# Later fetches for v and the routing constants, and half of the first k copies moved to VectorE

## Chip, cores and metric

The kernel runs on one core of a Trainium2 chip. The metric is the time of one execution on the device in microseconds (us); smaller is better.

## What is computed

Three layers in a row, on a batch of B=4 sequences of S=576 rows.

```python
# 1. attention: 8 heads of 64; heads 0-3 see 32 earlier rows, heads 4-7 every fourth of 128 earlier rows
scores = where(mask[h], q @ k.T / sqrt(64), -1e9)
x = softmax(scores) @ v                      # heads side by side: [B, S, 512]
# 2. mixture of experts: one of 8 experts per row, chosen by a gate
logits = x @ w_gate; local = sigmoid(x @ w_local)
e[s] = argmax(logits[s]) if s == 0 or local[s] < 0.5 else e[s-1]
x[s] = softmax(logits[s])[e] * (relu(x[s] @ w1[e]) @ w2[e])     # 512 -> 1024 -> 512
# 3. last layer: convolution over 5 rows as a gate
gate = sigmoid(sum(conv_w[k] * shifted(x, 4 - k)))
out = (gate * (x @ w_val)) @ w_out
```

## The kernel before

The attention is cut into eight **items**, `it` 0 to 7. An item is one pair of heads for two sequences (`bl` 0 and 1). Items 0 and 1 are heads 0 and 1, then 2 and 3, of sequences 0 and 1; item 2 is the first pair of the strided heads. An item is cut into five **groups**, and the outer loop (L1041) counts groups, `t` = 5 * `it` + `gi`. Within one `t` the work of several groups is interleaved in a hand-written order; each engine runs its instructions strictly in that order, so whatever stands behind a waiting instruction on the same engine waits too.

For one group: `stage_a` multiplies q by a block-diagonal k (`kbd`) on TensorE into PSUM (tile `s`, L561) and VectorE adds the mask and takes the row maximum (`sm`, `mx`, L569); `stage_sub` subtracts the maximum on GpSimd (L577); `stage_exp` is on ScalarE (L584); two groups later `stage_b` transposes the result (`pt`, `ph`); three later `stage_c` multiplies by v (`o`, L630), and the result goes to `xsb`. `stage_d` and `stage_l` transpose it (`tpx`) and accumulate the gate's logits (`lp`).

Ahead of an item its q and k must be transposed. `load_qk(it, bl)` issues one transfer for q (`qraw`) and one for k (`kraw`), 288 KB each, on SyncE's queue, SP. `side` packs q for the transposes (`qside`), on VectorE for items 0 and 1 (L480) and on GpSimd from item 2 on (L482), in two halves for each `bl`. `qraw` has two buffers, so a transfer for one item waits until `side` has read the one two transfers before it. `transpose_qk` transposes eight units per item: for q, VectorE copies PSUM to `qT` (L531, L529); for k, ScalarE makes two copies per unit, one for even rows (`e` = 0) and one for odd (`e` = 1), from the two halves of the PSUM partitions into `kbd` (L545, L542). Item 0's units 0 to 3 are made before the loop, 4 and 5 at `t` = 0 and 6 and 7 at `t` = 1; the k units are 2, 3, 6 and 7, so item 0 has eight k copies.

v is loaded by `load_v`, a generator with one transfer at each step: for heads 0 to 3 of a sequence four transfers of 144 KB, one for each head. Before the loop heads 0 and 1 of sequences 0 and 1 are sent; heads 2 and 3 are put into the list `vq`, from which `send` takes up to six transfers a group at `t` % 10 < 2 and four otherwise. Their first readers are `shift_v` of item 1 on ScalarE at `t` = 6 and 9 and `stage_c` of item 1. The constants come in four parts (`consts_in`); part 2 holds the masks of the strided heads and is fetched at `t` = CONSTS[0], part 3 holds the routing's constants, 933 columns of 4 bytes on 128 partitions or 466.5 KB, and is fetched at `t` = CONSTS[1]. `tables` is a generator that makes three sets of tables from part 3 on VectorE: `triu` and `lane` (L197, L198), then `lanes` (L200), then `cols` and `sv` (L202, L203); one set is made at each `t` in PREP. The routing that reads them starts at `t` = START = 25.

`busy(n)` issues n matmuls of no use, to keep TensorE at work: 40 at the start and FILL[0] and FILL[1] after k units 1 and 3. Some ten lines of the loop set the order on SP; at the end of one `t` it is:

```python
if t == 2:
    load_qk(2, 0)
if (gi == 1 and it and it + 2 < 8) or t == 3:
    load_qk(it + 2, 1)
...
if gi == 3 and it + 3 < 8:
    load_qk(it + 3, 0)
for n in (2, 3):
    if t == CONSTS[n - 2]:
        consts_in(nc.sync, n)
if t in PREP:
    next(prep, None)
...
left = send(vq, 6 if t % 10 < 2 else 4)
```

After the attention the experts' matmuls and the last layer follow; they are not touched.

Of the kernel before, what the change touches and what calls it, by code (L numbers as in the profile page):

```python
# [50 lines left out]
TILES = 5  # L51
VB = 3
BUSY = 40
FILL = (6, 16)
SPLIT = ((33, 34), (33, 34), (34, 36), (37, 38), (38, 39), (39, 42), (41, 43), (41, 42), (45, 46), (47, 48), (48, 50), (51, 52), (52, 57), (55, 59), (57, 61), (61, 63))
GATHERS = (37, 38, 38, 40)
TURNS = (39, 40, 40, 43)
UP = (42, 43, 44, 44, 45, 46, 46, 47)
EXPERT2 = 33
CONSTS = (4, 7)  # L60
LATE = ((0, 1, 0, 1, 0, 1, 0, 1, 0, 1, 0, 1, 0, 1, 0, 1), (1, 1, 1, 1, 1, 1, 1, 2, 1, 1, 1, 1, 1, 1, 1, 2), (1, 1, 1, 1, 1, 1, 1, 1, 1, 1, 1, 1, 1, 1, 1, 1), (0, 1, 1, 1, 1, 1, 1, 1, 0, 1, 1, 1, 1, 1, 1, 1), (0, 1, 1, 0, 1, 1, 0, 1, 1, 0, 1, 1, 0, 1, 1, 1), (0, 1, 0, 1, 0, 1, 0, 1, 1, 0, 1, 0, 1, 0, 1, 1), (0, 0, 1, 0, 1, 0, 1, 0, 0, 1, 0, 1, 0, 1, 0, 1))
RINGS = ((1, 1), (2, 1), (2, 3), (3, 0), (1, 0), (2, 0), (0, 0), (0, 0))
PREP = (10, 18, 22)
PLACES = (1, 0, 0, 2)
EVACUATE = 2
START = 25
# [93 lines left out]
def attention_moe_conv_kernel(ctx: ExitStack, tc: tile.TileContext, q, k, v, w_gate, w_local, w1, w2, w_val, conv_w, w_out, consts, out):  # L160
    nc = tc.nc
    V, A, G, T = nc.vector, nc.scalar, nc.gpsimd, nc.tensor
# [10 lines left out]
    def consts_in(eng, n):  # L173
        eng.dma_start(out=cst[:, cuts[n] : cuts[n + 1]], in_=consts[:, cuts[n] : cuts[n + 1]])
# [253 lines left out]
    if True:  # L428
# [28 lines left out]
        def pair(it):  # L457
            return it // 4, PR[it // 4][it % 4]

        def load_qk(it, bl):  # L460
            bp, pr = pair(it)
            b = 2 * bp + bl
            for nm, src in (("q", q), ("k", k)):
                tj, tp = TJ[pr >= 2], TP[pr >= 2]
                r = ld.tile([tp, 2, tj, HD], F32, tag=f"{nm}raw", name=f"{nm}raw{it}_{bl}", bufs=2 if nm == "q" else 4)
                rows = src[b, 2 * pr : 2 * pr + 2].rearrange("h (p j) d -> p h j d", j=tj)
                nc.sync.dma_start(out=r, in_=rows)
                raw[it, bl, nm] = r
# [40 lines left out]
        def psum(ring, it, shape, nm):  # L509
            pool, tag = ((trp, "tr"), (pp, "pt"), (sp, "s"), (op, "o"))[ring[it == 7]]  # L510
            return pool.tile(shape, F32, tag=tag, name=nm)

        def transpose_qk(it, unit):
            bp, pr = pair(it)
            bl, n2, jj = unit // 4, (unit // 2) % 2, unit % 2
            nm = "qk"[n2]
            if unit == 0:
                qk[it] = (qt.tile([P, 2, S], F32, tag="qT", name=f"qT{it}"), kbd[it % 2])
            dil = pr >= 2
            tj, tp = TJ[dil], TP[dil]  # L520
            hj = tj // 2
            ps = psum(RINGS[6 + n2], 0 if jj == 0 else 7, [P, hj, tp], f"tp{nm}{it}_{unit}")
            qT, (kb, _) = qk[it]
            if nm == "q":
                for rr in range(hj):
                    T.transpose(ps[:, rr, :], sides[it, bl][:, hj * jj + rr, :], ident[:tp, :tp])
                t = qT[:, bl, :]
                if dil:
                    V.tensor_copy(out=t.rearrange("c (r p two) -> c r p two", r=4, two=2)[:, :, :, jj], in_=ps)  # L529
                else:  # L530
                    V.tensor_copy(out=t.rearrange("c (p j) -> c p j", j=tj)[:, :, hj * jj : hj * jj + hj], in_=ps.rearrange("c r p -> c p r"))  # L531
                later.tick()
                return
            h = jj
            for m in range(hj):
                T.transpose(ps[:, m, :], raw[it, bl, "k"][:, h, 2 * m : 2 * m + 2, :].rearrange("p e d -> p (e d)"), ident[:tp, :tp])
            t = kb[HD * h : HD * h + HD, bl, h, :]
            for e in range(2):
                half = ps[HD * e : HD * e + HD]
                if dil:  # L540
                    to = t.rearrange("c (m e p two) -> c e two m p", m=2, e=2, two=2)[:, e]
                    A.copy(out=to, in_=half.rearrange("c (two m) p -> c two m p", two=2))  # L542
                else:
                    to = t.rearrange("c (p m e) -> c e p m", m=hj, e=2)[:, e]
                    A.copy(out=to, in_=half.rearrange("c m p -> c p m"))  # L545

        def scores(nm):
            return sp.tile([P, 2, 2, KB], F32, tag="s", name=nm)
# [451 lines left out]
        vq, xq, evs, xs = [], [], {}, [[], []]  # L1000
# [9 lines left out]
        def v_of(m):  # L1010
            b, dil = 2 * (2 * (m // 2) // 4) + m % 2, pair(2 * (m // 2))[1] >= 2
            return load_v(b, dil)

        with tc.manual_schedule():
# [4 lines left out]
            v0, v1 = v_of(0), v_of(1)  # L1019
# [1 line left out]
            send([v1], 2)  # L1021
            load_qk(1, 0)
            load_qk(1, 1)
            vq += [v0, v1]

            def busy(n):
                ps = op.tile([P, P], F32, tag="o", name="busy")
                for _ in range(n):
                    T.matmul(ps, lhsT=ones16, rhs=ones16, start=True, stop=True)
# [4 lines left out]
            for u in range(4):  # L1034
                transpose_qk(0, u)
                if u % 2:
                    busy(FILL[u // 2])
            for half in range(2):
                side(0, 1, half)
            prep = tables()  # L1040
            for t in range(NG + 5):  # L1041
                it, gi = divmod(t, 5)
                if t < NG:
                    stage_a(t)
                    if t < 2:
                        for u in (4 + 2 * t, 5 + 2 * t):
                            transpose_qk(0, u)
                    elif t < 5:
                        for u in ([0, 1], [2, 3], [4, 5, 6, 7])[t - 2]:
                            transpose_qk(1, u)  # L1050
                    elif it + 1 < 8:
                        for u in units[gi]:
                            transpose_qk(it + 1, u)
                    stage_sub(t)
# [35 lines left out]
                    nc.gpsimd.dma_start(out=wg[:, :, E : E + 1], in_=w_local.rearrange("(c p) e -> p c e", p=P))  # L1090
                if t == 2:
                    load_qk(2, 0)
                if (gi == 1 and it and it + 2 < 8) or t == 3:
                    load_qk(it + 2, 1)
                if gi in (1, 2) and it + 2 < 8 and it:
# [9 lines left out]
# [5 lines that stand above are left out]
# [518 lines left out]
```

## Time and profile before

| | us |
|---|---|
| median of three executions | 461.28 |
| the three | 460.99, 461.28, 463.59 |
| the profiled execution, its own time | 462.0 |
| its span, first to last instruction | 460.2 |
| TensorE busy in the span | 436.9 (95%) |
| VectorE busy | 345.0 (75%) |
| ScalarE busy | 289.5 (63%) |
| GpSimd busy | 164.8 (36%) |

The span is what the trace shows; 1.8 us of the profiled execution lie around it. Busy shares are means over stages with different limits, and a busy TensorE is not one at its peak. In the rows below PE is TensorE's matmuls, PEld its weight loads, DVE VectorE, ACT ScalarE, POOL GpSimd, and SPq SyncE's queue that issues transfers. Times are us from the start of the span, and a bracket at the end of a row gives how long the engine stood idle before it and what ended that.

### The profile page before, as it was taken

The page shows a single profiled execution, that of the slowest core. Times are in us where ns is not written, and L with a number is a line of the kernel's source. Part 1 is how long each engine was busy: PE and PEld are TensorE (multiplying, and loading weights), DVE is VectorE, ACT ScalarE, POOL GpSimd, SP SyncE. Part 2 cuts the span into 40 slices and gives each one's busy share as a digit, 9 for nine tenths or more (in the row PEclk, how much of TensorE's full clock was granted, in tenths as well). Part 3 has the DMA queues.
Part 4 walks back from the last instruction along what each step waited for, and adds up shares of the span by engine and source line. Part 5 has one row for each costly group of instructions (what it writes and reads, how often), then busy time and mean ns, then how long its engine had stood idle before and what let it go on. Part 6 is the DMA issues. An engine that isn't in the chain of part 4 may idle for free. (4 is left out here: it accounts for less than half of the span.)

```text
span 460.2 us, 12124 instructions
## 1 busy us (share of the span) xinstructions
PE 436.9 (95%) x4618; PEld 325.5 (71%) x4618; DVE 345.0 (75%) x1015; ACT 289.5 (63%) x581; POOL 164.8 (36%) x192
## 2 busy tenths in 40 slices
PE   8799999888789999999999999999999999999997
PEld 7567777666466578875788888788785857666664
DVE  5767688989878883787979898997138788779730
ACT  2877887667745233546666657767447998785532
POOL 3565665421700252302313232252005655334130
PEclk9999999989989999999999999999999999999999
DMA  9978698446648475277858897981053323020202
GB/s 209 204 166 203 137 241 208 134 118 223 199 121 279 161 271 181 67 214 274 283 158 298 276 308 254 326 275 60 11 154 100 126 71 125 25 91 1 93 20 95
DMA packets 56868, 77.79 MB, mean 169 GB/s; under 512 B 25809, under 2 KB 34017, under 8 KB 56806
## 3 DMA queue, kind: packets, MB, share of 16 engines
q1 hardware_dynamic: 53430, 67.18, 49.2%
q0 software_dynamic: 3232, 9.72, 6.2%
q8 instruction: 38, 0.62, 0.6%
q14 instruction: 24, 0.20, 0.1%
q10 hardware_dynamic: 144, 0.07, 0.1%
HBM read 62.65 MB, written 14.30 MB: 167 GB/s over the span
## 5 line engine op out<-in xcount | busy, mean ns | idle before, releaser
L346 PE MATMUL h<-xh,wh 128*128 128x256 f16 (+9 forms) x352 | 86.4, 256 | 2.4 <-DVE hl L350 2.2
L346 PE MATMUL h<-xl,wh 128*128 128x256 f16 (+9 forms) x352 | 86.4, 256 | 0.1
L346 PE MATMUL h<-xh,wl 128*128 128x256 f16 (+9 forms) x352 | 86.4, 256 | 0.0
L268 DVE SCALAR_TENSOR_TENSOR wl<-wst,wh 128x1024 f16<-128x1024 f32 x64 | 77.8, 1219 | 10.0 <-ACT wh L263 9.9
L1475 DVE SCALAR_TENSOR_TENSOR acc<-y,cw,acc 128x288 f32<-128x288 f32 x128 | 65.6, 520 | 9.2 <-ACT acc L1449 6.3
L346 PEld LDWEIGHTS <-wh 128*128 128x128 f16 x704 | 64.2, 98 | 10.6 <-issue 4.1
L263 ACT ACTIVATE wh<-wst 128x1024 f16<-128x1024 f32 x64 | 67.0, 1051 | 2.9 <-DMA wst<-in_moe_w_dram 2.8
L348 ACT ACTIVATE hh<-h 128x256 f16<-128x256 f32 (+9 forms) x88 | 30.7, 348 | 42.5 <-PE h L346 39.9
L577 POOL TENSOR_TENSOR sm<-sm,mx 128x384 f32<-128x384 f32 (+1 forms) x40 | 33.0, 824 | 52.8 <-DVE mx L569 37.0
L350 DVE SCALAR_TENSOR_TENSOR hl<-h,hh 128x256 f16<-128x256 f32 (+9 forms) x88 | 32.3, 375 | 25.0 <-ACT hh L348 24.5
L357 POOL DMA_INDIRECT yD<-yr,sidx x15 | 18.2, 1216 | 84.2 <-ACT yr L356 56.5
L395 PE MATMUL yf<-wh,hh 128*128 128x512 f16 x104 | 39.4, 379 | 0.1
L395 PE MATMUL yf<-wl,hh 128*128 128x512 f16 x104 | 39.4, 379 | 0.0
L395 PE MATMUL yf<-wh,hl 128*128 128x512 f16 x104 | 39.4, 379 | 0.0
L1505 PE MATMUL v<-yh,wv_h 128*128 128x288 f16 x128 | 36.6, 286 | 0.3 <-DVE gg L1514 0.2
L1505 PE MATMUL v<-yh,wv_l 128*128 128x288 f16 x128 | 36.6, 286 | 0.0
L1505 PE MATMUL v<-yl,wv_h 128*128 128x288 f16 x128 | 36.6, 286 | 0.0
L346 PEld LDWEIGHTS <-wl 128*128 128x128 f16 x352 | 34.4, 98 | 2.5 <-issue 0.2
L569 DVE CUSTOM_DVE_ANT_0 sm<-s,cst 128x96 f32<-128x96 f32 x144 | 29.7, 250 | 7.7 <-PE s L561 5.1
L395 PEld LDWEIGHTS <-hh 128*128 128x128 f16 x208 | 20.3, 98 | 21.1 <-issue 0.6
L379 PEld LDWEIGHTS <-wh 128*128 128x128 f16 x576 | 32.9, 97 | 2.2
L561 PE MATMUL s<-kbd,qT 128*64 128x192 f32 x288 | 31.7, 332 | 2.8 <-ACT kbd L545 2.0
(259 smaller groups left out, 1061.5 us busy)
## 6 DMA issues: line engine op xcount, KB each, us to landing
wst<-in_moe_w_dram SPq DMA_DIRECT2D x64, 512.0 KB
qraw<-in_q_dram SPq DMA_DIRECT2D x16, 288.0 KB
kraw<-in_k_dram SPq DMA_DIRECT2D x16, 288.0 KB
out_dram<-ob SPq DMA_DIRECT2D x17, 256.0 KB
yg<-yD SPq DMA_DIRECT2D x16, 256.0 KB
xD<-xsb SPq DMA_DIRECT2D x2, 1152.0 KB
lraw<-in_moe_w_val_dram SPq DMA_DIRECT2D x4, 512.0 KB
lraw<-in_moe_w_out_dram SPq DMA_DIRECT2D x4, 512.0 KB
```

Source lines behind the costliest of these rows:

```text
L263: A.activation(out=wh, in_=st, func=AF.Copy, scale=SW)
L268: V.scalar_tensor_tensor(out=wl, in0=st, scalar=SW, in1=wh, op0=ALU.mult, op1=ALU.subtract)
L346: T.matmul(ps[:, :n], lhsT=w[:, fs], rhs=x[:, cc, :], start=q == 0, stop=q == 11)
L348: A.activation(out=hh[:, fc, :], in_=ps[:, :n], func=AF.Relu)
L350: V.scalar_tensor_tensor(out=hl[:, fc, :], in0=ps[:, :n], scalar=0.0, in1=hh[:, fc, :], op0=ALU.max, op1=ALU.subtract)
L379: T.matmul(ps[:, :r], lhsT=w[:, ds_], rhs=x[:, fc, r0:n], start=q == 0, stop=q == 23)
L395: T.matmul(ps, lhsT=x[:, fc, t0 : t0 + P], rhs=w[:, (fc % 2) * D : (fc % 2) * D + D], start=q == 0, stop=q == 23)
L561: T.matmul(ps[64 * half : 64 * half + 64, n, :, :], lhsT=qf[:, QB * blk : QB * blk + QB], rhs=kb[:, bl, :, ks[i] : ks[i] + KB] if i else f ...
L569: V.tensor_tensor_reduce(out=sm[:, n, h, :], in0=ps[:, n, h, :], in1=cst[:, o + KB * mi : o + KB * mi + KB], scale=0.125, scalar=-3e38, op ...
L577: G.tensor_tensor(out=smf, in0=smf, in1=mx[:, 0 : 2 * ns].unsqueeze(2).to_broadcast([P, 2 * ns, KB]), op=ALU.subtract)
L1475: V.scalar_tensor_tensor(out=acc, in0=y32[:, cc, s0 + k : s0 + k + hw], scalar=cw[:, cc, k : k + 1], in1=acc, op0=ALU.mult, op1=ALU.add)
L1505: T.matmul(ps, lhsT=w[:, cc, cs], rhs=x[:, cc, hs], start=q == 0, stop=q == 11)
```

## The change

Half of item 0's k copies, those with `e` = 1, are made by VectorE in place of ScalarE. Six of the useless matmuls behind unit 3 go. The transfers for v of heads 2 and 3 join the list at `t` = 2, right after `load_qk(2, 0)`, and no longer before the loop (where the list was first served at the end of `t` = 0). Part 3 of the constants is fetched at `t` = 12 and not 7. The tables `triu` and `lane` are made at `t` = 18 and not 10, and `lanes` at 20 and not 18; `cols` and `sv` stay at 22.

```diff
-FILL = (6, 16)
+FILL = (6, 10)
...
-CONSTS = (4, 7)
+CONSTS = (4, 12)
...
-PREP = (10, 18, 22)
+PREP = (18, 20, 22)
...
             for e in range(2):
                 half = ps[HD * e : HD * e + HD]
+                copy = V.tensor_copy if it == 0 and e else A.copy
                 if dil:
...
-                    A.copy(out=to, in_=half.rearrange("c (two m) p -> c two m p", two=2))
+                    copy(out=to, in_=half.rearrange("c (two m) p -> c two m p", two=2))
                 else:
...
-                    A.copy(out=to, in_=half.rearrange("c m p -> c p m"))
+                    copy(out=to, in_=half.rearrange("c m p -> c p m"))
...
             load_qk(1, 0)
             load_qk(1, 1)
-            vq += [v0, v1]
...
                 if t == 2:
                     load_qk(2, 0)
+                    vq += [v0, v1]
```

## Rows read from the trace of the kernel before

**Rows 1.** Busy time by stage, items 1 to 4: from:to, length, busy (count), clock, DMA share, GB/s

```profile
21.10:36.17 15.07, 13.34 (x192) 9.76 (x187) 9.38 (x54) 10.89 (x23) 10.26 (x14) 1.00 0.74 172
36.17:49.66 13.49, 13.10 (x190) 9.59 (x187) 9.76 (x55) 10.26 (x22) 9.24 (x14) 1.00 0.78 187
49.66:61.90 12.24, 12.24 (x189) 9.49 (x186) 10.50 (x54) 10.27 (x21) 6.80 (x8) 1.00 0.59 140
61.90:74.40 12.50, 12.50 (x193) 9.57 (x191) 10.08 (x55) 10.24 (x21) 8.63 (x14) 1.00 0.92 237
```

**Rows 2.** The waits of TensorE in item 1: in total, times, longest

```profile
PE tpq L526 <- POOL qside L482: 1.3, 3, 0.5
```

**Rows 3.** Timeline of GpSimd, 19 to 27 us: start, length, instruction, idle before

```profile
19.08 0.51 POOL L577 TENSOR_TENSOR sm<-sm,mx 128x192 f32<-128x192 f32 x1 [0.30 <-DVE mx L569]
21.29 2.04 POOL L482 TENSOR_TENSOR qside<-qraw,one 72x512 f32<-72x512 f32 x2 [1.71 <-DMA qraw<-in_q_dram]
24.86 1.04 POOL L482 TENSOR_TENSOR qside<-qraw,one 72x512 f32<-72x512 f32 x1 [1.53 <-DMA qraw<-in_q_dram]
...
26.18 0.82 POOL L577 TENSOR_TENSOR sm<-sm,mx 128x384 f32<-128x384 f32 x1
```

**Rows 4.** Timeline of VectorE and TensorE, 41 to 60 us

```profile
41.57 0.19 DVE L197 CAST triu<-cst 72x72 f16<-72x72 f32 x1 [1.42 <-DMA cst<-in_consts_dram]
...
45.59 0.55 PE L642 MATMUL tpx<-cst,xsb 128*128 128x128 f32 x3 [0.40 <-DVE xsb L611]
...
59.36 1.53 DVE L200 TENSOR_SCALAR lanes<-cst 72x2048 f16<-72x2048 f32 x1
```

**Rows 5.** Timeline of the start, 5 to 14 us, compute engines

```profile
5.64 0.82 DVE L531 COPY qT<-tpq 128x288 f32<-128x288 f32 x2 [0.71 <-PE tpq L526]
...
6.66 1.69 ACT L545 COPY kbd<-tpk 64x288 f32<-64x288 f32 x4 [4.18 <-PE tpk L536]
...
6.82 1.06 PE L1029 MATMUL busy<-ones 128*128 128x128 f16 x16
...
8.40 0.87 PE L561 MATMUL s<-kbd,qT 128*64 128x192 f32 x8 [0.53 <-ACT kbd L545]
...
11.61 1.67 ACT L545 COPY kbd<-tpk 64x288 f32<-64x288 f32 x4
...
12.49 0.36 DVE L480 COPY qside<-qraw 96x384 f32<-96x384 f32 x1 [1.63 <-DMA qraw<-in_q_dram]
...
13.33 0.86 PE L561 MATMUL s<-kbd,qT 128*64 128x192 f32 x6 [1.48 <-ACT kbd L545]
...
13.47 0.35 DVE L480 COPY qside<-qraw 96x384 f32<-96x384 f32 x1
```

**Rows 6.** Timeline of SP's queue: issues, each with its length

```profile
0.75 0.39 SPq L467 DMA_DIRECT2D qraw<-in_q_dram  x1
...
11.05 4.18 SPq L492 DMA_DIRECT2D vraw1False<-in_v_dram  x2
15.33 1.50 SPq L467 DMA_DIRECT2D qraw<-in_q_dram  x1
```

**Rows 7.** Busy time by stage around the first transfers; columns as in rows 1

```profile
2.00:15.00 13.00, 10.99 (x113) 9.07 (x111) 7.08 (x37) 5.80 (x12) 3.69 (x12) 1.00 1.13 250
18.00:24.00 6.00, 4.39 (x53) 3.36 (x52) 3.98 (x20) 4.39 (x9) 3.33 (x4) 1.00 0.82 187
```

**Rows 8.** Busy time by stage and granted clock; columns as in rows 1

```profile
12.00:15.00 3.00, 1.67 (x15) 1.35 (x16) 2.10 (x19) 2.75 (x6) 0.88 (x1) 1.00 1.14 251
15.50:18.50 3.00, 3.00 (x43) 2.24 (x40) 2.54 (x15) 2.43 (x6) 2.79 (x4) 1.00 1.13 188
124.00:127.80 3.80, 1.60 (x22) 1.01 (x20) 2.52 (x5) 2.72 (x5) 2.49 (x3) 1.00 0.89 277
128.00:131.00 3.00, 3.00 (x22) 2.60 (x24) 1.71 (x4) 1.60 (x4) 0.00 (x0) 0.50 0.38 138
```

**Rows 9.** Timeline of TensorE in a stretch at half clock, 93.8 to 97.2 us

```profile
93.65 1.39 PE L561 MATMUL s<-kbd,qT 128*64 128x192 f32 x8
```

## The prediction

> **What bounds the kernel now.** I read the busy time by stage first, cut where the scores of each item begin [rows 1]. Items 3 and 4 take 12.24 and 12.50 us, and TensorE is busy in all of it: that is the pace of this loop when nothing else holds it up. Item 1 takes 15.07 us with TensorE busy for 13.34, so it stands 1.73 us and runs 2.83 us over the pace of item 3; item 2 takes 13.49 us, 1.25 over. From 49.66 us on there is no slack for early fetches to win, and TensorE-bound stages only pass on what they get. So the change can win at most what lies ahead of 49.66: 2.83 + 1.25 = 4.1 us in items 1 and 2, and something in item 0.
>
> Next, who holds up item 1. TensorE waits 1.3 us, in three pieces, for `qside` from GpSimd [rows 2]. GpSimd in turn waits 1.71 us for the first `qraw` of item 2 and, one piece later, 1.53 us for the second; the subtraction of group 5, which the exponent and the rest of that group need, stands behind them in GpSimd's order and starts only at 26.18 [rows 3]. Item 1 is thus paced by the landing of the second `qraw` of item 2, at about 24.8 us. In item 2 VectorE stands 1.42 us before `triu`, for the routing's constants, with all mask work of the next groups behind it; three groups later TensorE stands 0.40 us for VectorE's `xsb` [rows 4].
>
> **Half of the k copies, first time (units 2 and 3).** Now ScalarE makes four copies in 1.69 us, from 6.66 to 8.35, and the first scores start at 8.40 [rows 5]. VectorE is free at 6.46, after two `qT` copies of the same 288 columns in 0.82 us, the nearest row for a k copy on it: 0.41 us each, as on ScalarE. With two copies on each engine k is there at about 7.5, or at 8.0 if the second copy of a unit has to wait for the first. Ten useless matmuls in place of sixteen take 1.06 x 10 / 16 = 0.66 us from 6.82 and end at 7.48, so they don't stand in the way. The scores start 0.4 to 0.85 us sooner. What is late next: VectorE's `qside` piece of item 1 waits 1.63 us, until 12.49, for a transfer that this change doesn't move [rows 5]. The gain is shorter than that wait: worth 0.
>
> **Half of the k copies, second time (units 6 and 7).** Here the edit costs something. ScalarE now makes these copies from 11.61 to 13.28, early, and the rest of group 2's scores starts at 13.33 [rows 5]. On VectorE two of them stand behind the `qside` piece that waits for its transfer (12.49) and behind the mask work of group 1, which ends at about 13.47, where the next `qside` piece starts. So they run from 13.47 to 14.3, k is complete 1.0 us later than now, and group 2's scores start at about 14.35. Queued behind them on VectorE is that next `qside` piece, which ends at 14.65 and not at 13.82. Groups 2 to 4 move back by 1.0 us. I take all of it as a loss at group 5, and nothing of it at group 6, because there TensorE now waits about 1 us for the first `qside` pieces of item 2 [rows 2], and these come earlier, as follows.
>
> **v behind q and k.** SP now issues the four v transfers from 9.73 us on (the last two take 4.18 us, up against a full queue), and the first `qraw` of item 2 only at 15.33 [rows 6]. After the change SP has nothing to do until the `qside` piece frees its buffer at 14.65; it then issues q and k of item 2, `bl` 0, then the four v transfers, and then, because the list is served at the end of `t` = 2, q and k of `bl` 1 at `t` = 3. The first `qraw` loses 4 x 144 KB = 0.59 MB ahead of it, 2.4 us at 250 GB/s [rows 7]; it was there at 21.29 and will be there before GpSimd asks for it, at about 19.6 + 1.0 us [rows 3]. But the second `qraw`, which paces item 1, still has the same bytes ahead of it, in another order. Its landing can only move by what the queue loses by running dry. Sent before it: 8 x 288 + 208 + 4 x 144 = 3088 KB, or 3.16 MB, which at 250 GB/s from 2.0 us is through at 14.6 [rows 7], just when the next transfer is issued. From issue to first bytes I estimate 1.3 us, from the first issue at 0.75 and a stretch from 2.00 on that is already full [rows 6 and 7]. So the landing moves by 0 to +1.3 us. The low end is nearer: by mean rates the first `qraw` ought to be there at 2.0 + 3.75 / 0.25 = 17.0, plus 295 KB at 187 GB/s, 18.6, and the trace has 21.29; the slowest of the engines that share a transfer, which sets the landing, is over 2 us behind the mean and doesn't run dry. I take +0.3. The v data lands before that `qraw`, so before `shift_v` of group 6 reads it.
>
> **The constants and tables.** `triu` and `lane` no longer stop VectorE in item 2: 1.42 us of waiting and two casts go. What it gives is bounded by item 2's excess, 0 to -1.25 us; I take -1.0, since TensorE's wait three groups later is for VectorE and what remains is the lag of ScalarE behind it. The 466.5 KB move from a stretch with a DMA share of 0.78 to one with 0.59 [rows 1]: 2 us of transfer, in idle time; what waits behind it on SP is item 5's q, wanted two groups later; 0. `triu` and `lane` at `t` = 18 cost 0.4 us of VectorE where 1.53 us of `lanes` stood; `lanes` goes to `t` = 20, where VectorE is busy for 10.08 of 12.50 us and will be for 11.6 [rows 1, 4]. Beside TensorE at its pace that is nearly hidden: +0.2, at most +1.1, the price that a stall of similar length had in item 2.
>
> **Sum.** 0 (first copies) + 0 (second copies, absorbed) + 0.3 - 1.0 + 0.2 = -0.5 us. The profiled execution would go from 462.0 to 461.5 us, its span from 460.2 to 459.7. It ran 0.7 above the median of the three, so I forecast the median: 461.28 - 0.5 = 460.8.
>
> One thing speaks against the change that the sum doesn't hold. TensorE will have nothing to do from about 11.0 to 14.35 us, where now it stands 1.48. The granted clock fell to 0.50 of full, 1.2 GHz, after a stretch with 1.60 of 3.80 us busy, and stayed at 1.00 after one with 1.67 of 3.00 [rows 8]. At half clock a set of scores takes 1.39 us and not 0.87 [rows 5 and 9]; over one such stretch that is some 1.4 us for groups 2 to 4, and up to group 6 it is covered in the same way as the 1.0 above, all but about 0.5. The Trainium skill ("TensorE: Matmul & The Clock Gate", Part 1) says that an idle TensorE is gated back to half its clock and that activity releases it. By that rule the stretch after 14 us would run at 1.2 GHz and the sum would be 0.0 instead of -0.5; by the stretch at 12 us, which was not followed by a fall, it stays at -0.5. No row yet shows a gap this long.
>
> **Rivals.** (a) *Faster: item 1's wait goes.* If the second `qraw` lands well before 24.8 us, item 1 runs at pace. Group 5 then starts 1.0 later, at 22.1, and items 1 and 2 take 12.3 each: 46.7 in place of 49.66, -2.9, or -3.9 if the second copies also cost nothing: 457.4 to 458.4. For it: the transfers share engines and the queue is shallower. Against it: the four v transfers still come first on SP. (b) *Slower: the queue runs dry.* The full 1.3 us is paid at the second `qraw`; it decides as soon as it exceeds the 0.8 that the constants give. Item 1 pays 1.3, the rest as forecast: +0.5; with the fall of the clock or the full price of `lanes`, up to +2.1: 461.8 to 463.4. For it: the bytes sent and the free buffer meet at 14.6 within 0.1 us. Against it: the 2 us that the slowest engine lags. (c) *It doesn't do what it says:* v is fetched later but nothing that paces the loop is fetched sooner, and VectorE's stall was hidden: 461.3.
>
> **Chances.** Forecast (460.0 to 461.2) 0.45; (a) 0.23; (b) 0.22; (c) 0.10. For 8 in 10 the range takes in (a) and (b) almost to their ends: 457.6 to 463.4. A change of 1%, 4.6 us, is about what can be told from none here. Faster by that would need more than all of the excess of items 1 and 2: 0.07. Slower by it would need two of the costs at twice their bound: 0.05. Within 1%: 0.88.
>
> **What would show it.** Right: first scores at 7.5 to 8.0, group 2's at about 14.3, no wait of GpSimd for the first `qraw` of item 2, its wait for the second ending at 24.7 to 26, item 1 no shorter than 14 us, item 2 near 12.5, items 3 and 4 as now within 0.3. Wrong: the second `qraw` there at 23, or group 5 not later than 21.2; a longer item 4 would show `lanes` uncovered, and a clock of 0.50 around 15 us the idle TensorE.

## The result, and the profile after

The changed kernel takes 465.98 us (median of 13 executions, 461.42 to 467.55) against 461.56 us (median of 13, 460.94 to 465.58): a ratio of 1.0083, with an interval of 1.0056 to 1.0110. The forecast was 460.8 us, and 465.98 lies 2.6 us above its range. The profiled execution took 467.55 us with a span of 465.8, so it is the slowest of the thirteen; what it shows is one execution's case, and the two further profiles of the same kernel below are needed to say how far it holds. The ratios here leave out disturbed executions, so they may differ a little from the ratio of two medians.

Busy time by stage of the changed kernel, cut where the scores of items 1 to 5 begin, with the columns of [rows 1]:

```profile
21.71:40.43 18.72, 16.01 (x189) 11.82 (x187) 9.58 (x53) 10.94 (x23) 9.57 (x13) 0.82 0.78 180
40.43:53.44 13.01, 12.99 (x189) 9.56 (x187) 9.46 (x53) 10.55 (x22) 8.41 (x13) 1.00 0.46 103
53.44:65.73 12.29, 12.29 (x190) 9.54 (x188) 9.86 (x55) 10.11 (x21) 6.79 (x8) 1.00 0.67 160
65.73:78.72 12.99, 12.65 (x189) 9.57 (x187) 11.96 (x56) 9.87 (x21) 8.19 (x14) 1.00 0.93 245
```

Item 1 takes 18.72 us and not 15.07 [rows 1], at a mean granted clock of 0.82. Item 2 is 0.48 shorter, item 3 equal, item 4 0.49 longer. So up to item 5 the loss lies in items 0 and 1, 4.3 us, and is then passed on. From there to the end of the span another 1.2 us are lost (387.0 against 385.8); "What stays open" comes back to that. Two views show where the loss of items 0 and 1 comes from. First SyncE's queue (start, length, issue):

```profile
14.60 0.36 SPq L467 DMA_DIRECT2D qraw<-in_q_dram  x1
15.05 0.30 SPq L467 DMA_DIRECT2D kraw<-in_k_dram  x1
15.40 1.27 SPq L492 DMA_DIRECT2D vraw0False<-in_v_dram  x2
16.72 1.50 SPq L492 DMA_DIRECT2D vraw1False<-in_v_dram  x2
18.32 1.69 SPq L467 DMA_DIRECT2D qraw<-in_q_dram  x1
```

and the transfers' own view of 13 to 17 us in 40 slices of 0.1 us (busy tenths, then GB/s):

```profile
DMA  9999999999876410101101000995233567666899
GB/s 261 261 230 277 364 292 276 246 292 230 215 200 154 92 31 0 15 0 15 15 0 15 15 0 31 179 154 97 77 123 143 184 246 287 246 246 266 328 287 197
```

From 14.4 to 15.5 us almost nothing moves: what was sent has landed, and SyncE stood until 14.57 for the buffer of item 2's first q. In the kernel before transfers run through that stretch without a gap [rows 7, 8]. What it costs is read on GpSimd, in the rows that answer to [rows 3]:

```profile
20.23 2.03 POOL L482 TENSOR_TENSOR qside<-qraw,one 72x512 f32<-72x512 f32 x2
26.32 1.04 POOL L482 TENSOR_TENSOR qside<-qraw,one 72x512 f32<-72x512 f32 x1 [4.06 <-DMA qraw<-in_q_dram]
...
27.64 0.82 POOL L578 TENSOR_TENSOR sm<-sm,mx 128x384 f32<-128x384 f32 x1
```

The wait for the first q of item 2 is gone, as meant; the second q comes at 26.32 and not at 24.86, and behind it, at 27.64 and not at 26.18, the subtraction of group 5. ScalarE stands behind that:

```profile
28.48 0.52 ACT L585 ACTIVATE pb<-sm 128x384 f32<-128x384 f32 x1 [3.76 <-POOL sm L578]
28.91 1.68 ACT L543 COPY kbd<-tpk 64x288 f32<-64x288 f32 x4
```

And TensorE behind ScalarE, since the q and k transposes share two PSUM buffers that only these copies free (the first is done at 29.75; the row names `qside`, which had been done since 27.36):

```profile
11.42 0.54 PE L562 MATMUL s<-kbd,qT 128*64 128x192 f32 x2
14.24 0.86 PE L562 MATMUL s<-kbd,qT 128*64 128x192 f32 x6 [2.27 <-DVE kbd L546]
...
24.45 0.82 PE L562 MATMUL s<-kbd,qT 128*64 128x192 f32 x8
...
26.59 0.82 PE L562 MATMUL s<-kbd,qT 128*64 128x192 f32 x8
29.83 0.57 PE L526 MATMUL tpq<-cst,qside 72*128 72x72 f32 x4 [2.42 <-POOL qside L482]
...
33.32 1.50 PE L562 MATMUL s<-kbd,qT 128*64 128x192 f32 x8
...
37.42 0.50 PE L562 MATMUL s<-kbd,qT 128*64 128x192 f32 x4
...
40.49 0.82 PE L562 MATMUL s<-kbd,qT 128*64 128x192 f32 x8
```

The same places in the kernel before, TensorE:

```profile
28.38 0.44 PE L526 MATMUL tpq<-cst,qside 72*128 72x72 f32 x4 [0.34 <-POOL qside L482]
...
30.66 0.82 PE L561 MATMUL s<-kbd,qT 128*64 128x192 f32 x8
...
33.09 0.50 PE L561 MATMUL s<-kbd,qT 128*64 128x192 f32 x4
...
36.17 0.82 PE L561 MATMUL s<-kbd,qT 128*64 128x192 f32 x8
```

Groups 6 and 7 start 0.62 sooner than before (24.45 and 26.59 against 25.07 and 27.21), so TensorE comes sooner to the wait of group 7, and it is released 1.45 later (29.83 against 28.38): 2.42 us in one piece, where before it had stood 0.34. From then on it is slow: a set of scores takes 1.50 in place of 0.82. The granted clock shows why. Busy time and clock in two stretches of the changed kernel, one behind the wait of 2.27 us at group 2, one behind that of 2.42 at group 7:

```profile
14.30:17.70 3.40, 3.40 (x33) 2.58 (x34) 2.83 (x14) 1.16 (x3) 1.68 (x2) 1.00 0.59 142
...
30.00:36.80 6.80, 6.51 (x42) 5.01 (x41) 3.05 (x14) 4.46 (x9) 3.84 (x5) 0.50 0.58 140
```

Group 10 thus starts 4.32 us later (40.49 against 36.17): 1.45 by the release, 1.21 between the transposes and group 8 (33.32 - 29.83 against 30.66 - 28.38), 1.67 between groups 8 and 9 (4.10 against 2.43). Some 1.45 is the late transfer and 2.9 the low clock.

### The profile page after: what moved, and what is told of

It reads as the page before. It is cut to its first block, busy times and chain, and to the rows that moved or that the text cites. A ratio compares the mean times of both kernels' runs of the same rounds, so it can differ in the third digit from the quotient of the medians.

```text
span 465.8 us, 12114 instructions
## 1 busy us (share of the span) xinstructions
PE 441.3 (95%) x4612; PEld 328.5 (71%) x4612; DVE 348.0 (75%) x1019; ACT 287.8 (62%) x577; POOL 166.2 (36%) x192
## 3 DMA queue, kind: packets, MB, share of 16 engines
HBM read 62.65 MB, written 14.30 MB: 165 GB/s over the span
```

## The experiments

Theory Q, formed from that profile: the emptied queue, the late second q, and the half clock behind the wait that it makes, in every execution. Rival K: the k copies on VectorE, which move group 2 back, are the cause. Rival C: the constants' tables in item 4. After the first four runs theory L took the place of Q: TensorE has two long waits, at groups 2 and 7, and behind either the clock may fall or not. Each kernel ran 12 times, in sets of up to four kernels on one chip; the ratios are to runs of the kernel before in the same set.

**Each part alone, and all but one.** The v move alone (e1):

```diff
 load_qk(1, 1)
-vq += [v0, v1]
...
 load_qk(2, 0)
+vq += [v0, v1]
```

> The kernel before with only the v transfers moved. Theory Q (the transfer queue runs empty from 14 to 15.6 us, the second q of item 2 lands 1.5 us later, TensorE stands over 2 us for it and then runs at half clock): second q of item 2 at 26.0 to 26.5 us, scores of group 8 at 32.5 to 33.5 instead of 30.6, granted clock 0.50 in item 1, time 464.5 to 467. Rival K (the k copies on VectorE, with group 2 at 14.2 instead of 13.3, are the cause): 461 to 462. Rival C (the constants' table in item 4 is the cause): 461 to 462.

The changed kernel with the v transfers back in their place (e2; the two lines the other way round):

> The changed kernel with the v transfers back in their old place; k copies and constants stay changed. Theory Q: no empty queue, second q of item 2 at 24.5 to 25.0 us, group 8's scores at 30.5 to 31, clock 1.00 in item 1, time 460.5 to 461.8. Rival K: 464 to 466. Rival C: item 4 stays at 13.0 us and carries most of it, 464 to 466.

The k copies with the ten fillers (the useless matmuls of `busy`) alone (e7), and the constants alone, that twice (e8, e14):

> The kernel before with the k copies and the ten fillers alone. Theory L: group 2 at 14.2, lull 2.3 us or more, half clock behind it in part of the executions, then 2 us later by group 5; 0.5 to 2.5 us slower than before. Theory Q (only the v move starves the queue): no slower than before, 461.5 to 463.

> The kernel before with the later constants and tables alone. Forecast of this part: item 2 shorter by 0.5 to 1.0 us, item 4 longer by 0.2 to 0.6, so 0.3 to 0.8 us faster up to item 5. If group 28's start at 86.4 us is set by something that no earlier start moves (it was at 86.3 to 86.5 in three kernels whose item 5 started at 73.2 to 74.3), nothing of that reaches the end: ratio 0.997 to 1.003.

> The kernel before with the later constants and tables alone, a second time, on another chip perhaps. If this part is worth what its first profile showed (item 2 shorter by 0.5, item 4 longer by 0.1): ratio 0.996 to 1.000. If the first ratio of 0.9968 was chance: 0.999 to 1.003.

**The changed kernel unaltered** (e5, e9), as the yardstick of two of the sets:

> The changed kernel, unaltered, beside the same runs of the kernel before as the experiments, as their yardstick. Theory Q (a late second q of item 2 in every run): again 1.006 to 1.011 times the kernel before, second q at 26.0 to 26.5. Theory L (the change makes the lull of TensorE at 11.4 to 14.2 us longer, and after a long lull some executions run a stretch at half clock, others don't; the late second q of the first profile was one execution's): the ratio is smaller, 1.002 to 1.008, the second q lands between 24.3 and 26.5, and either the first or the second lull shows half clock behind it.

> The changed kernel once more, as the yardstick of the three kernels beside it. Theory L (a longer lull of TensorE at group 2, a second one at group 7 when the second q of item 2 is late; behind either, some executions run at half clock): one of the two stretches at 0.50 in the profile, group 10 at 36 to 41 us, times in two clumps some 3 to 4 us apart, median 0 to 4 us over the kernel before.

**The clock.** Useless matmuls in TensorE's waits; in the first (e3) only at group 7, in the second (e11) also at group 2:

```diff
 elif it + 1 < 8:
+    if t == 7:
+        busy(34)
     for u in units[gi]:
         transpose_qk(it + 1, u)
...
 for u in (4 + 2 * t, 5 + 2 * t):
     transpose_qk(0, u)
+if t == 1:
+    busy(34)
```

> The changed kernel with 34 useless matmuls (about 2.2 us) in TensorE's order ahead of the transposes of group 7, where it stands for 2.4 us. Theory Q: the second q still lands at 26.3 and group 8 is still 1.5 us late, but the granted clock stays at 1.00, so that group 8's scores start at about 32.0, item 1 takes 15.5 to 16.2 us instead of 18.7, and the time is 462.5 to 463.5. Rival (the low clock is an accompaniment that costs nothing, or comes from the wait for data itself): 465 to 467.

> The changed kernel with 34 useless matmuls (2.2 us) in each of TensorE's two lulls, behind the k transposes of group 1 and ahead of the transposes of group 7. Theory L: granted clock 1.00 from 6 to 40 us, group 3 at 16.0 to 16.3, group 5 at 21.6 to 21.8, group 10 at 34.6 to 37.5 by where the second q lands; median 1 to 3 us under the changed kernel. Rival (the low clock has nothing to do with TensorE's lulls): half clock there as before, no gain, or a loss of up to 1 us by the fillers.

**The queue and the copies.** The buffer freed sooner (e4):

```diff
-if t in (0, 1):
-    side(1, 0, t)
+if t == 0:
+    side(1, 0, 0)
+    side(1, 0, 1)
```

> The changed kernel with the second piece of item 1's first q copied right behind the first one, at about 12.5 us instead of 14.2, so that the buffer for item 2's first q is free 1.7 us sooner. Theory Q: SyncE issues that q at about 12.9 instead of 14.6, the queue doesn't run empty, the second q of item 2 lands at 24.3 to 25.0, no half clock in item 1, time 460.0 to 461.8. Rival K: it puts 0.35 us more ahead of the masks of group 1 and takes nothing away, 465.5 to 467. If only the order of bytes counts (v ahead of the second q), it also stays at 465 to 466.

VectorE copies only the first two units of k (e6); both edits are in the two kernels after that (e10, and e12 with v in its old place):

```diff
-copy = V.tensor_copy if it == 0 and e else A.copy
+copy = V.tensor_copy if it == 0 and bl == 0 and e else A.copy
```

> The changed kernel with the k copies on VectorE only for the first two units; the later two units stay with ScalarE. Theory L: group 2's scores at 13.3 instead of 14.2, the lull before them 1.5 us, no half clock behind it, buffer for item 2's first q free at 13.8 instead of 14.6, time 1.5 to 3 us under the changed kernel on the same chip. Theory Q: the queue is empty for 0.7 us less, gain 1 to 4 us as well, but then through the second q's landing (24.3 to 25.0). Rival C (constants' table): no gain, within 0.5 us of the changed kernel.

> The changed kernel with VectorE copying only the first two units of k, and both pieces of item 1's first q copied at 12.5 us, which frees its buffer 1.7 us sooner. Theory L: neither lull is left (group 2 at 13.4, second q of item 2 before 24 us), so no half clock in items 0 to 2, item 1 at its pace (12.7 to 12.9), group 10 at 33.7 to 34.2 instead of 36.1, 2 to 3.5 us faster than the kernel before. Rival (transfers pace item 1 whatever is done): group 10 at 35.5 to 36.5, within 1 us of before.

> The same as the version with two copies and the buffer freed sooner, but with the v transfers in their old place. If the v move is worth something: the second q of item 2 waits behind v as in the kernel before (24.1 to 24.8), group 10 at 35.2 to 35.8, 1 to 2 us slower than with the v move. If not: within 0.5 us of it.

And those two edits with 24 useless matmuls ahead of group 7's transposes (e13):

> The version with two copies on VectorE and the buffer freed sooner, with 24 useless matmuls (1.6 us) ahead of the transposes of group 7, where TensorE stood 1.1 us and ran at half clock behind it. Theory L: granted clock 1.00 from 6 to 40 us, group 7's step at most 3.8 us instead of 4.7 and the next at 2.45 instead of 3.50, group 10 at 35.0 to 35.6 instead of 37.0, 1 us sooner than in the kernel before; group 25 at 72.8 to 73.5. Rival (the clock falls whatever TensorE does): 0.50 near 30 us and group 10 at 37 or later.

**Measured.** Of each kernel's profile: TensorE's wait at group 2 and the clock behind it; the start of the second `qside` piece of item 2 on GpSimd; TensorE's wait at group 7 and the clock behind it; the start of groups 5, 10 and 25. Then the median, that of the kernel before beside it, and the ratio with its interval. "-" is a wait under 0.15; (f) is what is left behind fillers.

| kernel | wait, clock at 2 | second q | wait, clock at 7 | group 5 | group 10 | group 25 | median / before | ratio |
|---|---|---|---|---|---|---|---|---|
| before | 1.48, 1.00 | 24.86 | 0.34, 1.00 | 21.12 | 36.17 | 74.39 | | |
| changed | 2.27, 1.00 | 26.32 | 2.42, 0.50 | 21.76 | 40.49 | 78.78 | 465.98 / 461.56 | 1.0083 (1.0056 to 1.0110) |
| e5, changed | 2.98, 0.50 | 24.96 | -, 1.00 | 23.55 | 36.34 | 74.14 | 463.11 / 463.40 | 1.0010 (0.9967 to 1.0052) |
| e9, changed | 2.62, 1.00 | 26.77 | 2.40, 0.50 | 22.24 | 40.93 | 78.74 | 464.88 / 463.84 | 1.0018 (0.9986 to 1.0051) |
| e1, v only | 1.48, 1.00 | 24.45 | 1.18, 1.00 | 21.14 | 35.76 | 73.88 | 461.49 / 462.58 | 0.9993 (0.9954 to 1.0031) |
| e2, all but v | 2.31, 1.00 | 24.14 | 0.33, 1.00 | 21.70 | 35.48 | 73.28 | 462.91 / 462.58 | 0.9994 (0.9955 to 1.0034) |
| e7, copies only | 2.42, 0.50 | 25.06 | -, 1.00 | 23.32 | 36.41 | 74.56 | 464.52 / 463.40 | 0.9992 (0.9950 to 1.0033) |
| e8, constants only | 1.50, 1.00 | 24.91 | 0.71, 1.00 | 21.73 | 36.22 | 74.02 | 462.62 / 463.40 | 0.9968 (0.9929 to 1.0007) |
| e14, the same | 1.5, 1.00 | 24.88 | 0.7, 1.00 | 21.85 | 36.20 | 74.36 | 461.14 / 461.78 | 0.9993 (0.9960 to 1.0026) |
| e3, filled at 7 | 2.94, 0.50 | 25.41 | -, 1.00 | 23.70 | 38.35 | 77.09 | 463.72 / 462.58 | 1.0022 (0.9991 to 1.0052) |
| e11, filled at both | 0.45 (f), 1.00 | 26.14 | 0.17 (f), 1.00 | 21.83 | 37.46 | 77.44 | 467.45 / 463.84 | 1.0086 (1.0048 to 1.0124) |
| e4, buffer sooner | 2.96, 0.50 | 24.3 | -, 1.00 | 23.79 | 36.58 | 74.38 | 462.31 / 462.58 | 1.0005 (0.9977 to 1.0033) |
| e6, two copies | 1.35, 1.00 | 25.28 | 2.03, 0.50 | 21.11 | 38.12 | 76.15 | 466.06 / 463.40 | 1.0039 (1.0003 to 1.0075) |
| e10, both | 1.34, 1.00 | 24.21 | 1.10, 0.50 | 20.98 | 37.06 | 75.08 | 465.84 / 463.84 | 1.0020 (0.9985 to 1.0055) |
| e12, both, v as before | 1.35, 1.00 | 24.82 | 0.40, 1.00 | 21.44 | 36.14 | 73.94 | 463.50 / 463.84 | 1.0002 (0.9965 to 1.0039) |
| e13, both, filled at 7 | 1.3, 1.00 | 25.51 | 1.20 (f), 1.00 | 20.73 | 36.81 | 75.34 | 462.24 / 461.78 | 1.0001 (0.9973 to 1.0028) |

**What follows.** Rival C is out: the constants alone cost nothing in either set. Rival K alone is out as well: the copies alone gave 0.9992. But so did the v move alone, 0.9993. That the loss belongs to the two together is not shown: by their times e5 and e9, the changed kernel itself, can't be told from none either. In the profiles the long wait at group 7 goes with the v move. Without half clock at group 2 and without fillers it is 1.10 to 2.42 us in the five profiles with v moved (changed, e1, e6, e9, e10) and 0.33 to 0.71 in the five with v in its old place (before, e2, e8, e12, e14).

The late copies seem to add to it. With the v move alone the second piece of item 1's q follows its first by 1 us on VectorE; with the copies between them, by 2.1 us (12.13 and 14.21 in the changed kernel), and the buffer comes free behind it. In the five profiles with v moved, late copies and the buffer freed in the old order (changed, e3, e5, e9, e11) the second q's piece starts at 24.96 to 26.77, mean 25.92; in the five others with v moved, at 24.21 to 25.51, mean 24.7; in the six with v in its old place (before, e2, e7, e8, e12, e14), at 24.14 to 25.06, mean 24.78. So the longer stop of the queue is worth about 1.1 us on the mean, and no single landing proves it. In e1 SyncE issued item 2's first q at 14.30, only 0.3 sooner than in the changed kernel, and nearly as little was moved between 13 and 17 us (0.72 MB against 0.66), but the second q was there at 24.45. In e13 the queue didn't run empty (0.93 MB), and the second q came at 25.51.

Theory Q fell first with e1, where v alone was moved and neither the late q nor the half clock came, and then with e5. That is the changed kernel, and it reached group 25 at 74.14, before the kernel before. Its TensorE rows and the busy time behind the wait:

```profile
14.44 1.52 PE L562 MATMUL s<-kbd,qT 128*64 128x192 f32 x6 [2.98 <-DVE kbd L546]
15.89 1.22 PE L526 MATMUL tpq<-cst,qside 96*128 96x96 f32 x6
17.90 0.87 PE L562 MATMUL s<-kbd,qT 128*64 128x192 f32 x8
...
23.55 0.82 PE L562 MATMUL s<-kbd,qT 128*64 128x192 f32 x8
```

```profile
14.50:17.90 3.40, 3.40 (x16) 2.31 (x17) 1.89 (x11) 0.52 (x2) 1.02 (x2) 0.50 0.55 144
```

Here the half clock came behind the first wait. It put group 5 at 23.55; by then the second q (24.96) was nearly there, TensorE had no second wait, and item 1 ran at its pace. The early loss was covered, helped by a q that came 1.4 us sooner than in the first profile; the late one in the other two profiles wasn't. This is theory L, and the table bears it out: behind an unfilled wait of 2.3 to 3.0 us at group 2 the clock was 0.50 in four profiles of seven, behind waits of 1.3 to 1.5 in none of eight; at group 7, behind waits of 1.1 to 2.42, 0.50 in four of five, behind 0.3 to 0.7 in none. e3 was meant as the test of it, but its profile had the half clock behind group 2 and no wait left to fill at group 7, where its fillers then cost about 2 us (group 10 at 38.35 against 36.34 in e5). In e4 the second q was there by 24.3, as expected, but half clock stood behind a wait of 2.96 at group 2. e11 is the direct test, though of one profile: the second q came as late as in the changed kernel (26.14), but with TensorE busy in both waits.

```profile
27.42 2.07 PE L1029 MATMUL busy<-ones 128*128 128x128 f16 x34
29.66 0.44 PE L526 MATMUL tpq<-cst,qside 72*128 72x72 f32 x4 [0.17 <-issue]
...
31.95 0.82 PE L562 MATMUL s<-kbd,qT 128*64 128x192 f32 x8
...
37.46 0.82 PE L562 MATMUL s<-kbd,qT 128*64 128x192 f32 x8
```

```profile
27.40:29.60 2.20, 2.09 (x36) 1.90 (x34) 0.80 (x8) 1.25 (x4) 2.20 (x4) 1.00 0.91 210
29.60:33.00 3.40, 2.91 (x35) 2.34 (x36) 1.68 (x5) 3.31 (x7) 3.24 (x4) 1.00 0.39 80
33.00:36.40 3.40, 3.40 (x51) 2.18 (x49) 1.90 (x14) 3.08 (x8) 1.60 (x3) 1.00 0.75 204
```

The scores of group 8 take 0.82, and group 10 starts at 37.46, 3.0 us before that of the changed kernel and 1.3 behind the kernel before: the late transfer without the low clock. e10 is the converse. Its second q is there at 24.21, sooner than before, and its wait only 1.10, yet the clock fell:

```profile
27.73 0.44 PE L526 MATMUL tpq<-cst,qside 72*128 72x72 f32 x4 [1.10 <-POOL qside L482]
...
30.54 1.49 PE L562 MATMUL s<-kbd,qT 128*64 128x192 f32 x8
```

```profile
29.40:32.70 3.30, 3.30 (x25) 2.26 (x24) 1.54 (x9) 2.07 (x5) 1.51 (x2) 0.50 0.40 73
```

So the rival of e10, that transfers pace item 1 whatever is done, fell too: its groups 5 to 7 were the earliest of those without fillers, and it lost that behind the wait. e6 has the same end: group 2 at its old time, a wait of 2.03 at group 7, half clock, and nothing of the 1.5 to 3 us that were expected. e12, with v in its old place and so with short waits, has no stretch at half clock in items 0 to 4 and is the equal of the kernel before. Neither of its expectations came: its group 10, at 36.14, is 0.9 us ahead of that of e10, whose clock fell. e13 fills part of the wait; its clock stayed at 1.00 although its second q came 1.3 us later than that of e10, and its twelve times lie at 459.1 to 464.0. Its group 10, at 36.81, missed the expected 35.0 to 35.6 by that landing.

**What the fillers didn't give.** e11 gained 3 us by group 10 and is the slowest kernel of all. Its profile lost part of it again in item 4, where the logits' matmul ahead of group 25 waits (GpSimd stood 1.7 us for a q of item 6 there), and TensorE stood for its own sequencer in the expert stage, at a place where no other profile shows a stop:

```profile
75.96 0.46 PE L655 MATMUL lp<-xT,wg 128*32 128x144 f32 x8 [0.98 <-ACT xT L644]
...
330.12 0.38 PE L395 MATMUL yf<-wh,hh 128*128 128x512 f16 x1 [1.42 <-PEq L1335]
```

Whether the 68 further matmuls cause that stop was not tried. No version was found that beats the kernel before beyond its interval; the constants alone come nearest, at 0.9968 and 0.9993.

**What stays open.** Only the profiled executions show which wait was followed by half clock. The times of the changed kernel lie in two clumps, 461.4 to 463.5 (4) and 465.3 to 467.6 (9) in the first set, 462.1 to 463.1 (7) and 465.6 to 468.5 (5) in the second, less clearly in the third; the profile without the late stretch (e5, 463.12) lies in the lower, the two with it (467.55 and 468.48) in the upper. That the other executions divide in the same way is not shown. In the second set the kernel before spreads as widely, over 460.5 to 468.7, and the rest of the program can do the same: from group 25 to the end of the span the sixteen profiles take 383.6 (e3) to 390.3 us (e10), and between 80 and 150 us the mean granted clock is below 1.00 in every one, 0.88 to 0.98. One place shows it with the same wait in all sixteen, 1.39 to 1.41 us for the routing ahead of `wp`: in e1, e2, e5 and e13 the next scores take 0.85 or 0.86, in the others 0.50. The kernel before, then e1:

```profile
84.88 0.47 PE L789 MATMUL wp<-dg,ones 72*72 72x144 f32 x2 [1.40 <-DVE dg L700]
...
86.55 0.50 PE L561 MATMUL s<-kbd,qT 128*64 128x192 f32 x4
```

```profile
84.38 0.47 PE L789 MATMUL wp<-dg,ones 72*72 72x144 f32 x2 [1.40 <-DVE dg L700]
...
86.41 0.86 PE L561 MATMUL s<-kbd,qT 128*64 128x192 f32 x4
```

The profiled execution of e1 took 464.71 us without any half clock in items 0 to 4. So one time doesn't tell where the clock fell. These scores are group 29, which the expectation of e8 calls 28; their start isn't fixed at 86.4 us, e8 had 86.19. Why the first set had more of the upper clump, and so a loss of 0.8% where the other two can't be told from none, is not known.

## Why the prediction was wrong

**The second landing** is the step that failed first. The prediction gave it "0 to +1.3 us", held that "the low end is nearer" because the slowest engine "doesn't run dry", and took +0.3. In this profile it was +1.46, over five profiles about +1.1. The terms were there (the free buffer at 14.65, measured 14.57; the bytes through at 14.6, the queue empty from 14.4 to 15.5), and the high end followed from them; the argument from the lagging engine outweighed a coincidence that the text itself had worked out to 0.1 us. Rival (b) had the mechanism, as far as the means above show it.

**The half clock** is the step that made up the rest. The prediction looked for it only behind the lull of group 2, where it would have been covered "all but about 0.5", and so it was: e5 and e7 lost 2.2 to 2.4 us by group 5 and reached group 10 0.2 late. It took that lull for 11.0 to 14.35 us, but by [rows 5] the scores ahead of it end at 11.85 (13.33 less 1.48), and 2.27 us were measured. It did not ask what the absorbed waits become. "Nothing of it at group 6, because there TensorE now waits about 1 us" was right, group 6 started 0.62 sooner; but GpSimd still held group 5 back behind the second q, so the waits that had lain in pieces of 0.44, 0.53, 0.34 and 0.42 us before were gathered into one of 2.42, late in item 1 where nothing covers it. Even the dearest case of rival (b), 463.4, held only one covered stretch. The stretch at group 7, for which the sum had no term, cost 2.9 us. In the sum's terms this profile has +1.46 for the landing, +2.9 for the clock, -0.48 and +0.49 for the constants: 4.4 us, and group 25 starts 4.39 later, where -0.5 was forecast.

The Trainium skill ("TensorE: Matmul & The Clock Gate", Part 1) says that an idle TensorE is gated to half its clock and that activity releases it. The wait of group 7 agrees (0.50 behind 2.42 us); the prediction drew the rule on for the earlier wait alone, behind which it held in four profiles of seven.

**What is passed on.** The prediction held that from 49.66 us on stages only pass on what they get. They do up to group 25. Behind it they don't: e2 started group 25 1.1 us sooner than the kernel before, and group 29 at the same time (86.54 against 86.55), behind half clock. A gain of 0.5 us couldn't be seen in the time.

**The first copies.** Forecast: scores at 7.5 to 8.0. They start at 8.52, 1.45 after the first copy (7.07) and not 1.74 (6.66 to 8.40 in [rows 5]). VectorE's copies of the changed kernel, and its rows further on:

```profile
7.51 0.95 DVE L546 COPY kbd<-tpk 64x288 f32<-64x288 f32 x2 [0.64 <-ACT kbd L546]
...
13.23 0.95 DVE L546 COPY kbd<-tpk 64x288 f32<-64x288 f32 x2
14.21 0.36 DVE L480 COPY qside<-qraw 96x384 f32<-96x384 f32 x1
...
63.20 0.50 DVE L197 CAST triu<-cst 72x72 f16<-72x72 f32 x1
...
69.69 1.78 DVE L200 TENSOR_SCALAR lanes<-cst 72x2048 f16<-72x2048 f32 x1
```

VectorE waits for ScalarE's copy of the same unit, and two copies take 0.95, not 0.82: a gain of 0.3, worth nothing at the end, as forecast. **The second copies** came as worked out: 13.23 to 14.18 (13.47 to 14.3 forecast), group 2 at 14.24 (14.3), the `qside` piece done at 14.57 (14.65).

**The constants.** Forecast -1.0 in item 2 and +0.2 in item 4. Measured -0.48 and, in this profile, +0.49, with `lanes` at 1.78 us. In e8, where the part stands alone, item 2 also takes 13.01 and item 4 12.50, as long as before:

```profile
36.22:49.23 13.01, 12.99 (x191) 9.56 (x188) 9.51 (x53) 10.66 (x22) 9.26 (x14) 1.00 0.72 160
49.23:61.50 12.27, 12.27 (x189) 9.52 (x187) 9.79 (x56) 10.00 (x21) 6.80 (x8) 1.00 0.72 174
61.50:74.00 12.50, 12.47 (x190) 9.52 (x187) 11.45 (x56) 9.96 (x21) 8.33 (x14) 1.00 0.91 237
```

The mechanism was right, the first size half of what was said; item 2 keeps 0.77 us over the pace of item 3 that VectorE's stall does not explain. The gain of 0.4 to 0.5 us repeats: item 2 takes 13.00 to 13.02 us from the first scores to the next item's in all thirteen profiles with this part, and 13.40 to 13.49 in the three without (before, e1, e7). It is too small for either measurement of it. The +0.49 repeats only in part: item 4 takes 12.44 us in those three, 12.50 or 12.51 in six of the thirteen and 12.72 to 14.68 in the other seven, the most in e11, where the q of item 6 was late.

## What to carry to other kernels

A wait that is taken away at one place can come back at the next one that the same late datum holds up, and there in one piece: before a transfer is moved, add up what an engine's short waits become when they are gathered, and ask what TensorE's clock does behind that. When a transfer is put behind a buffer that has yet to come free, the time from "all sent" to "buffer free" can be lost (about 1.1 us here, on the mean), and an instruction that is put in front of the one that frees the buffer lengthens it. Where one profile shows a stretch at half clock, take a second and a third of the same kernel, and of the kernel before, ahead of building on it; and compare the start of one group with the same group's, since the time of an execution also holds what the clock did elsewhere.

## What the runs showed of the hardware that was not expected

TensorE's granted clock fell to 0.50 (1.2 GHz) after waits as short as 1.10 and 2.03 us in item 1, and stayed at 1.00 (2.4 GHz) after others of 1.18, 2.27 and 2.62 us: the same wait may or may not be followed by it, from one execution to the next. The wait of 1.40 us ahead of `wp` was followed by it in four profiles of sixteen. With useless matmuls in the wait at group 7 (TensorE busy 2.09 us of 2.20 in e11) it stayed at 1.00. In the trace VectorE's copy of half a unit of k out of PSUM started only when ScalarE had copied the other half of the same tile (7.51, after a start at 7.07 and 0.42 each), so dividing the copies between the two engines won 0.3 us of 1.7; whether the chip or the program's order of writes asks for that was not tried.
